# Sums of squares and output combinations by accumulating DMAs instead of VectorE additions

## The chip, the cores and the metric

The kernel runs on one core of one Trainium2 chip. The metric is the device time of one execution in microseconds (us); lower is better. A core has TensorE (PE, matmuls; its weight loads are listed as PEld), VectorE (DVE), ScalarE (ACT), GpSimd (POOL) and SyncE (SP), each with its own queue of instructions that it works off in order and with semaphores between them. Here SP issues all loads and stores; the DMA engines carry them out.

## The reference

Four batches of 6080 tokens with 256 channels go through an attention over channels and then through a two-layer network with squared ReLU:

```python
qn = q / (np.linalg.norm(q, axis=1, keepdims=True) + 1e-06)
kn = k / (np.linalg.norm(k, axis=1, keepdims=True) + 1e-06)
s = kn.transpose(0, 2, 1) @ qn / tau          # 256 x 256 per batch
a = np.exp(s - s.max(-1, keepdims=True))
a /= a.sum(-1, keepdims=True) + 1e-09
x = (v @ a).reshape(B * S, D)                 # (24320, 256)
h = np.maximum(x @ w_in, 0.0)                 # w_in: 256 x 2048
out = (h * h @ w_out).astype(np.float32)      # w_out: 2048 x 256
```

All of it is fp32. q, k and v are (4, 6080, 256).

## The kernel before

**Precision.** Every fp32 matrix is split into a high part and a low part (`_hi`, `_lo`), and a product is the sum of three: high by high, high by low, low by high. ScalarE makes the high part (a cast), VectorE the low part (the original minus the high part).

**Per batch: Gram matrix, softmax, folded weight.** `Gram` forms k^T q (tile `gram`) over chunks of tokens. A chunk is a tile `qk` of 128 partitions x (k or q) x 2 tokens x 256 channels, 128 x 1024 fp32 or 512 KB; with 6080 tokens there are 25 chunks: 0 to 22 are full, 23 has one token per partition, 24 has 64 partitions. The norms need the sums of squares of q and k over tokens. `squares` (ScalarE) squares a chunk, for later batches in place in its qk tile; `add_squares` adds the squares to the tile `acc`, chunk after chunk. `softmax_and_W` then adds acc's two halves (VectorE), sums them over the partitions by small matmuls (`ps_n`), forms the softmax, and multiplies it into w_in, which gives the folded weight `w_hi`, `w_lo` of the batch.

Batch 0 does this at the start (`start_first`). The first `HEAD = 6` chunks of batch 1 are loaded early and summed by `head_squares`. The rest of batch 1, and batches 2 and 3, run as the generator `attention(b)`, one piece of which is called per step of the main loop, beside the output blocks of the batch before. Per chunk it splits the qk tile into `qk_hi` and `qk_lo`, then calls `squares`, `add_squares` and, in the same piece, the load of the chunk after next (`g.load(c + QK_BUFS)`, `QK_BUFS = 2`): there are two qk buffers, so that load has to wait until the squares in the old chunk have been added. That is line 325 (k) and 326 (q) of the profile, on SP.

**Output blocks.** A batch's tokens are cut into 12 blocks, ten of 512 and two of 480. For a block there are 16 products with the folded weight (`first_product`: six matmuls into `ps_h`, then ScalarE's ReLU into `x`), two to a pair. `squares_and_sums` squares a pair (ScalarE), forms sums of quarters (VectorE) and splits them into `g_hi`, `g_lo`. Two pairs later `second_product` multiplies by w_out into `ps_o`. All blocks but the first two do it with seven products of half-size blocks instead of eight (`seven_products`), at the price of sums before and behind. The very last block does so for five of its eight pairs only (`SWITCH = 5`) and closes with plain products (`final_products`).

After a block's last pair, ScalarE copies the seven sums from `ps_o` into the tile `o` (128 x 7 x 256, one buffer, tag `o_sb`) in two copies, three slots and then four. `combine(b, n)` then turns the seven into the four quarters of the output, in five VectorE additions over three visits, and SP stores the quarters to `out_T` (line 841). The visits come from the list `late_work`, which the main loop looks at once per pair, before that step's `second_product`. For the last block the result stays in `o` for `final_products`.

**Order.** The main loop writes out by hand, step by step, what PE, VectorE, ScalarE and GpSimd get, and each keeps that order (`InProgramOrder`; so all their instructions have line 27). Semaphores and the order of SP's DMAs come from the framework: an instruction waits for whatever it reads or overwrites. GpSimd has nothing to do after setting up constants.

Of the kernel before, what the change touches and what calls it, by code (L numbers as in the profile page):

```python
# [14 lines left out]
ALU = mybir.AluOpType  # L15
# [15 lines left out]
def kernel(  # L31
# [21 lines left out]
    nc = tc.nc  # L53
    tensor, vector, scalar, pool_engine = (
        InProgramOrder(tc, e) for e in (nc.tensor, nc.vector, nc.scalar, nc.gpsimd)
    )
    P = 128
    B, N, C = q.shape
# [238 lines left out]
    HEAD = 6  # L297
# [3 lines left out]
    class Gram:  # L301
# [58 lines left out]
        def add_squares(self, c):  # L360
            p, jn, _ = self.q[c]
            if c in self.sq:
                a = self.acc[:p, :, :jn, :]
                vector.tensor_add(a, a, self.sq.pop(c)[:p, :, :jn, :])

    grams = {}

# [418 lines left out]
    def seven_products(b, n, r, part):  # L786
# [26 lines left out]
        if last:  # L813

            if part == 0:
                O[b, n] = pool.tile([P, 7, half], F32, tag="o_sb", name=f"o{b}_{n}", bufs=1)
            o, first = O[b, n], 1 - part
            scalar.copy(o[:, 3 * part : 3 * part + 4 - first, :], O.pop((b, n, part))[:, first:4, :half])
            if part:
                late_work.append(combine(b, n))  # L820

    def combine(b, n):

        t0, tn = blocks[n]
        half = tn // 2
        o = O.pop((b, n))
        both = lambda i: o[:, i : i + 1, :].broadcast_to([P, 2, half])
        vector.tensor_add(o[:, 1:4:2, :], o[:, 1:4:2, :], both(0))
        yield
        vector.tensor_add(o[:, 5, :], o[:, 5, :], o[:, 3, :])  # L830
        vector.tensor_add(o[:, 0, :], o[:, 5, :], o[:, 4, :])
        yield
        vector.tensor_add(o[:, 4, :], o[:, 4, :], o[:, 3, :])
        vector.tensor_add(o[:, 2:7:4, :], o[:, 2:7:4, :], o[:, 4:6, :])
        if (b, n) == order[-1]:
            final["sums"] = o
            return
        at = b * N + t0
        out = outT[:, at : at + tn].rearrange("(m p) t -> p m t", p=P)
        for m, k, slot in ((0, 0, 2), (0, 1, 1), (1, 0, 0), (1, 1, 6)):  # L840
            nc.sync.dma_start(out[:, m, k * half : (k + 1) * half], o[:, slot, :])
        yield

    late_work = []

    final = {}
# [68 lines left out]
    order = [(b, n) for b in range(B) for n in range(NB)]  # L915
# [20 lines left out]
    at = 0  # L936
# [13 lines left out]
    def then_sums():  # L950
        while grams[1].raws if B > 1 else False:
            yield
        yield from sums_of_w_out()

    sums = then_sums()
# [8 lines left out]
    for i in range(len(steps) + 2 * LAG):  # L964
        part = now["part"] = i % 2
        if i < len(steps):
            b, n, f = steps[i]
            at = b * NB + n
# [74 lines left out]
```

## Time and profile before

| | |
|---|---|
| timed runs | 2213.72 and 2215.77 us, median 2214.74 |
| span of the profiled execution, first to last instruction | 2211.6 us |
| PE busy | 2203.1 us |
| DVE busy | 1818.0 us |
| ACT busy | 1859.1 us |
| POOL busy | 0.7 us |
| DMA, mean | 67 GB/s |
| granted TensorE clock | 1.000 |

The page gives the profiled execution by its span; what lies around it, some 2 to 4 us by the timed runs, is not in the records. Busy time counts an engine's instructions but not the issuing of DMAs and the waiting for semaphores. A row of a group has line, engine, operation, tile written and tiles read, shapes, count, and then busy time, mean ns of one and the idle time in front of them. A row of a timeline has start, duration (both us), engine and operation. A row of DMAs has the size of one and the median time from its issue to its landing. A row of waits has who waited for whom, the total in us, how often, and the longest.

### The profile page before, as it was taken

What the parts mean: (1) busy time and instruction counts of PE and PEld (TensorE: products, weight loads), DVE (VectorE), ACT (ScalarE), POOL (GpSimd) and SP (SyncE); (2) the same over time, 40 slices, a digit from 0 to 9 for tenths busy, and PEclk for the clock granted to TensorE, in tenths of its full rate; (3) what the DMA queues carried; (4) which work ended last, traced back from release to release, by engine and by line L of the source; (5) the groups of instructions that cost most, each with busy time, mean ns of one, the idle gap of its engine ahead of it and who ended that gap; (6) DMA issues with size and microseconds to landing.
All of it is one profiled execution on the core that took longest, in us unless ns stands there. A gap on an engine that the chain in (4) does not pass through costs nothing.

```text
span 2211.6 us, 34981 instructions
## 1 busy us (share of the span) xinstructions
PE 2203.1 (100%) x13903; PEld 1985.0 (90%) x13903; DVE 1818.0 (82%) x2614; ACT 1859.1 (84%) x2347; POOL 0.7 (0%) x6
## 2 busy tenths in 40 slices
PE   9999999999999999999999999999999999999999
PEld 8789999988999999998999999999899988888898
DVE  6878888889888888878888888887888877787776
ACT  5788888888888888888878888888888888888887
POOL 0000000000000000000000000000000000000000
PEclk9999999999999999999999999999999999999999
DMA  9521122023421122210122122111103010010000
GB/s 342 179 77 39 61 77 65 27 76 109 157 86 58 60 62 71 63 60 21 36 95 86 60 66 76 58 53 60 33 24 115 22 36 20 22 37 20 20 28 19
DMA packets 82261, 148.03 MB, mean 67 GB/s; under 512 B 8368, under 2 KB 35760, under 8 KB 82096
## 3 DMA queue, kind: packets, MB, share of 16 engines
q1 hardware_dynamic: 82096, 145.79, 19.9%
q8 instruction: 109, 1.79, 0.3%
q14 instruction: 56, 0.46, 0.1%
HBM read 112.46 MB, written 33.29 MB: 66 GB/s over the span
## 4 chain that ended last, share of the span: by engine, by line
PE 92%; DVE 3%; DMA 2%; ACT 2%; issue 0%; SPq 0%; DVEq 0%; ACTq 0%
PE ps_h L27 46%; PE ps_o L27 41%; PE gram L27 4%; PE ps_w L27 2%; DMA qk<-in_k 1%; DVE g_lo L27 1%; DVE x L27 1%; ACT x L27 1%; DMA qk<-in_q 0%; DMA qk_heads<-in_q 0%; ACT g_hi L27 0%; DVE o L27 0%; DMA w_raw<-in_w_in 0%; DVE dec_m L27 0%; DMA wi_lo<-wi_kept 0%
## 5 line engine op out<-in xcount | busy, mean ns | idle before, releaser
L27 DVE TENSOR_TENSOR g_lo<-x,g_hi 128x768 fp32r<-128x768 f32 (+2 forms) x749 | 808.2, 1079 | 71.7 <-ACT g_hi L27 71.1
L27 DVE TENSOR_TENSOR x<-x 128x512 f32<-128x512 f32 (+1 forms) x1095 | 558.2, 510 | 244.0 <-ACT x L27 218.3
L27 ACT CAST g_hi<-x 128x768 fp32r<-128x768 f32 (+2 forms) x749 | 702.1, 937 | 42.8 <-DVE x L27 30.0
L27 ACT ACTIVATE x<-ps_h 128x512 f32<-128x512 f32 (+1 forms) x768 | 456.0, 594 | 248.7 <-PE ps_h L27 228.0
L27 PE MATMUL ps_h<-v_hi,w_hi 128*128 128x512 f32 (+1 forms) x1536 | 478.6, 393 | 0.0
L27 PE MATMUL ps_h<-v_hi,w_lo 128*128 128x512 f32 (+1 forms) x1536 | 477.9, 392 | 0.0
L27 PE MATMUL ps_h<-v_lo,w_hi 128*128 128x512 f32 (+1 forms) x1536 | 474.9, 390 | 0.0
L27 ACT ACTIVATE x<-x 128x1024 f32<-128x1024 f32 (+1 forms) x384 | 404.5, 1053 | 11.9
L27 PE MATMUL ps_o<-g_lo,wS_hi 128*128 128x256 f32 (+1 forms) x1460 | 407.6, 279 | 1.2 <-DVE g_lo L27 1.1
L27 PE MATMUL ps_o<-g_hi,wS_hi 128*128 128x256 f32 (+1 forms) x1460 | 406.1, 278 | 0.8 <-ACT o L27 0.8
L27 PE MATMUL ps_o<-g_hi,wS_lo 128*128 128x256 f32 (+1 forms) x1460 | 406.6, 278 | 0.0
L27 PEld LDWEIGHTS ps_h<-v_lo,w_hi 128*128 128x128 f32 x1536 | 287.9, 187 | 64.9
L27 PEld LDWEIGHTS ps_h<-v_hi,w_lo 128*128 128x128 f32 x1536 | 288.5, 188 | 62.4 <-DVE w_lo L27 0.3
L27 PE MATMUL ps_o<-g_hi,wo_hi 128*128 128x256 f32 (+2 forms) x1159 | 325.2, 285 | 0.6 <-ACT g_hi L27 0.6
L27 PE MATMUL ps_o<-g_hi,wo_lo 128*128 128x256 f32 (+2 forms) x1159 | 325.1, 285 | 0.0
L27 PE MATMUL ps_o<-g_lo,wo_hi 128*128 128x256 f32 (+2 forms) x1159 | 324.8, 285 | 0.1
L27 PEld LDWEIGHTS ps_o<-g_lo,wS_hi 128*128 128x128 f32 x1460 | 274.8, 188 | 17.9 <-DVE g_lo L27 2.1
L27 PEld LDWEIGHTS ps_o<-g_hi,wS_hi 128*128 128x128 f32 x1460 | 274.1, 188 | 17.2 <-ACT o L27 1.6
L27 PEld LDWEIGHTS ps_o<-g_hi,wS_lo 128*128 128x128 f32 x1460 | 274.4, 188 | 0.0
L27 PEld LDWEIGHTS ps_h<-v_hi,w_hi 128*128 128x128 f32 x1536 | 237.4, 188 | 3.6
L27 PEld LDWEIGHTS ps_o<-g_hi,wo_hi 128*128 128x128 f32 x1159 | 218.3, 188 | 15.7 <-ACT g_hi L27 1.0
L27 PEld LDWEIGHTS ps_o<-g_lo,wo_hi 128*128 128x128 f32 x1159 | 217.7, 188 | 15.2 <-DVE g_lo L27 0.5
(120 smaller groups left out, 1776.1 us busy)
## 6 DMA issues: line engine op xcount, KB each, us to landing
qk<-in_k SPq DMA_DIRECT2D x87, 256.0 KB, 2.8
qk<-in_q SPq DMA_DIRECT2D x87, 256.0 KB, 3.0
v<-in_vT SPq DMA_DIRECT2D x40, 512.0 KB, 3.8
out_T<-o SPq DMA_DIRECT2D x152, 128.0 KB, 1.7
wiS<-wi_sums_kept SPq DMA_DIRECT2D x24, 512.0 KB, 5.7
wi_hi<-wi_kept SPq DMA_DIRECT2D x16, 512.0 KB, 4.5
wi_lo<-wi_kept SPq DMA_DIRECT2D x16, 512.0 KB, 3.8
w_raw<-in_w_in SPq DMA_DIRECT2D x4, 1024.0 KB, 6.4
```

Of the source, the lines that this page charges most:

```text
L27: return lambda *args, **kwargs: self.tc.keep_in_program_order(issue(*args, **kwargs))
```

## The change

In batches after the first, `add_squares` for chunks from `HEAD` on no longer adds on VectorE: GpSimd issues a DMA from the squares (in the qk tile) to `acc` that adds to its destination. The first six chunks of every batch, and all of batch 0, stay on VectorE.

`combine` does the same for all blocks but the last: five accumulating DMAs within the tile `o`, issued by GpSimd over four visits, and the four stores in a fifth. The sums are arranged a little differently, so one output quarter ends in slot 5 instead of slot 0. The last block keeps the VectorE additions.

```diff
@@ add_squares @@
             if c in self.sq:
                 a = self.acc[:p, :, :jn, :]
-                vector.tensor_add(a, a, self.sq.pop(c)[:p, :, :jn, :])
+                if self.b == 0 or c < HEAD:
+                    vector.tensor_add(a, a, self.sq.pop(c)[:p, :, :jn, :])
+                else:
+                    pool_engine.dma_start(a, self.sq.pop(c)[:p, :, :jn, :], accum_op=ALU.add)
@@ combine @@
         both = lambda i: o[:, i : i + 1, :].broadcast_to([P, 2, half])
+        if (b, n) != order[-1]:
+            add = lambda at, what: pool_engine.dma_start(at, what, accum_op=ALU.add)
+            add(o[:, 1:4:2, :], both(0))
+            yield
+            add(o[:, 4, :], o[:, 3, :])
+            yield
+            add(o[:, 3, :], o[:, 5, :])
+            yield
+            add(o[:, 2:6:3, :], both(4))
+            add(o[:, 6, :], o[:, 3, :])
+            yield
+            at = b * N + t0
+            out = outT[:, at : at + tn].rearrange("(m p) t -> p m t", p=P)
+            for m, k, slot in ((0, 0, 2), (0, 1, 1), (1, 0, 5), (1, 1, 6)):
+                nc.sync.dma_start(out[:, m, k * half : (k + 1) * half], o[:, slot, :])
+            return
         vector.tensor_add(o[:, 1:4:2, :], o[:, 1:4:2, :], both(0))
         yield
         vector.tensor_add(o[:, 5, :], o[:, 5, :], o[:, 3, :])
...
         vector.tensor_add(o[:, 2:7:4, :], o[:, 2:7:4, :], o[:, 4:6, :])
-        if (b, n) == order[-1]:
-            final["sums"] = o
-            return
-        at = b * N + t0
-        out = outT[:, at : at + tn].rearrange("(m p) t -> p m t", p=P)
-        for m, k, slot in ((0, 0, 2), (0, 1, 1), (1, 0, 0), (1, 1, 6)):
-            nc.sync.dma_start(out[:, m, k * half : (k + 1) * half], o[:, slot, :])
-        yield
+        final["sums"] = o
```

## The prediction

> **What bounds the kernel now.** I read the page's busy line first, then the table of stretches, then what TensorE (PE) waited for.
>
> ```profile
> span 2211.6 us, 34981 instructions
> PE 2203.1 (100%) x13903; PEld 1985.0 (90%) x13903; DVE 1818.0 (82%) x2614; ACT 1859.1 (84%) x2347; POOL 0.7 (0%) x6
> ```
>
> PE is busy for all but 8.5 us of the span. VectorE (DVE), the engine that the change relieves, idles 18% of it, and GpSimd (POOL), which gets the new work, has six instructions in all. A busy PE could still be a slow one, so the next view is by stretch; its columns are the stretch, its length, the busy time of PE, PEld, DVE, ACT and POOL, the granted clock, the DMA share and GB/s.
>
> ```profile
> core 0: us, PE busy (x) PEld busy (x) DVE busy (x) ACT busy (x) POOL busy (x), PEclk, DMA share, GB/s
> 0.00:80.00 80.00, 77.25 (x344) 64.03 (x345) 60.05 (x78) 49.88 (x59) 0.70 (x6) 1.00 0.85 300
> ...
> 440.00:540.00 100.00, 98.06 (x618) 87.28 (x617) 88.92 (x153) 82.95 (x112) 0.00 (x0) 1.00 0.23 80
> ...
> 620.00:968.00 348.00, 348.00 (x2268) 316.13 (x2267) 296.08 (x402) 305.18 (x379) 0.00 (x0) 1.00 0.20 62
> ...
> 2170.00:2212.00 42.00, 37.75 (x231) 34.02 (x229) 24.39 (x38) 27.65 (x36) 0.00 (x0) 0.98 0.07 25
> ```
>
> Three stretches have PE idle: the start, 2.75 us (DMA share 0.85, and nothing of the change is there yet); 440 to 540, 1.94 us; and the end, 4.25 us, nearly all of it after the last matmul. In 620 to 968, a whole Gram stage with its squares, PE never stops, at clock 1.00. So VectorE can give back at most the middle one. What PE waited for after 80 us says the same:
>
> ```profile
> PE ps_o L27 <- DVE g_lo L27: 1.1, 2, 0.6
> PE ps_o L27 <- ACT o L27: 0.8, 2, 0.5
> ```
>
> Two waits on VectorE's low parts, two on ScalarE's copy of the output sums: 1.9 us together. This is the whole ceiling of a gain.
>
> **What goes from VectorE.**
>
> ```profile
> L27 DVE TENSOR_TENSOR acc<-acc,qk 128x1024 f32<-128x1024 f32 x63 | 76.9, 1221 | 12.2 <-ACT qk L27 12.2
> L27 DVE TENSOR_TENSOR o<-o 128x512 f32<-128x512 f32 x76 | 52.3, 688 | 1.3
> L27 DVE TENSOR_TENSOR o<-o 128x256 f32<-128x256 f32 x114 | 47.9, 420 | 1.3
> L27 DVE TENSOR_TENSOR o<-o 128x480 f32<-128x480 f32 x16 | 10.5, 655 | 0.3
> L27 DVE TENSOR_TENSOR o<-o 128x240 f32<-128x240 f32 x24 | 9.7, 403 | 0.3
> ```
>
> Of the 63 full chunk adds, chunks 6 to 22 of batches 1, 2 and 3 go: 17 x 3 = 51, by 1.221 us that is 62.3 us; the short chunks 23 and 24 of each batch go too, six adds of some 0.68 us, 4 us. Of the combinations, 46 blocks use seven products and only the last keeps its adds: all 76 and 114, 14 of 16 and 21 of 24, so 52.3 + 47.9 + 9.2 + 8.5 = 118 us. Together 184 us of 1818, which leaves VectorE at 1634 us, 74%. None of it is on the path outside 440 to 540, where the change removes about two blocks' adds (2 x 2.6 us). I credit half of the 1.94 us: **-1 us**.
>
> **What comes to POOL and the DMA engines.** 57 accumulations of squares and 45 x 5 of outputs, 282 DMAs. The trace has not one DMA issued by POOL and not one that accumulates, so their durations are bounded from SP's rows (size, us to landing):
>
> ```profile
> qk<-in_k SPq DMA_DIRECT2D x87, 256.0 KB, 2.8
> v<-in_vT SPq DMA_DIRECT2D x40, 512.0 KB, 3.8
> out_T<-o SPq DMA_DIRECT2D x152, 128.0 KB, 1.7
> w_raw<-in_w_out SPq DMA_DIRECT2D x4, 1024.0 KB, 5.4
> wi_sums_kept<-wiS_made SPq DMA_DIRECT2D x8, 512.0 KB, 2.6
> DMA to landing us min/median/max: 2.1/3.0/8.3
> ```
>
> (The last row is that of the qk tiles.) An accumulation reads source and destination, so I take the row with twice its bytes. A chunk of squares is 128 x 1024 fp32, 512 KB: between the 2.6 us of a plain store and the longest landing, 8.3 us; taken, as the 1 MB row, 5.4 us. A 256 KB step of the combination: 1.7 to 8.3, taken 3.8; a 128 KB step: 1.7 to 8.3, taken 2.8. The Trainium skill ("DMA: Bandwidth & Descriptors", Anatomy of one DMA, SWDGE path) fits a POOL-issued copy by 2.0 us plus bytes over 436 KB per us, which gives 3.2 us for 512 KB as an estimate; no run here shows one, and by it every cover below is wider still.
>
> *Squares.* What did take 1.22 us on VectorE now stands before a load, because the chunk after next lands in the buffer that the accumulation reads (two qk buffers). One of the closest places, ScalarE, VectorE and SP in turn:
>
> ```profile
> 676.02 1.05 ACT L27 CAST qk_hi<-qk 128x1024 fp32r<-128x1024 f32 x1
> 681.81 1.06 ACT L27 ACTIVATE qk<-qk 128x1024 f32<-128x1024 f32 x1
> 683.78 1.22 DVE L27 TENSOR_TENSOR acc<-acc,qk 128x1024 f32<-128x1024 f32 x1
> 685.02 0.34 SPq L325 DMA_DIRECT2D qk<-in_k  x1
> 685.41 0.42 SPq L326 DMA_DIRECT2D qk<-in_q  x1
> ...
> 699.87 1.04 ACT L27 CAST qk_hi<-qk 128x1024 fp32r<-128x1024 f32 x1
> ```
>
> The square ends at 682.87, the split of the chunk that this load brings starts at 699.87: 17.0 us. Two issues (0.8) and the landing (3.0) take 3.8, so 13.2 us are left for the accumulation; it needs 5.4, and if POOL stands first behind one combination step (3.8), 9.2. Cost nothing; without that cover each us would be ScalarE's, which is in order and has the next ReLU behind the split. Even 8.3 + 3.8 = 12.1 fits. SP waits longer at this load than before; behind it stand v loads and output stores, which have no deadline within a block (43 us by the copies below).
>
> *The new wait on VectorE.* At a batch's end the last, short accumulation (64 partitions) is followed by VectorE's sum of acc's halves, and behind that in its queue stand the low parts for PE.
>
> ```profile
> 430.85 0.62 ACT L27 ACTIVATE qk<-qk 64x512 f32<-64x512 f32 x1
> 438.04 0.68 DVE L27 TENSOR_TENSOR acc<-acc 128x512 f32<-128x512 f32 x1
> 440.36 0.28 PE L27 MATMUL ps_n<-ones,acc 128*128 128x1 f32 x2
> ```
>
> From the square's end, 431.47, to 438.04 are 6.6 us, for 128 KB (2.8). Cost nothing; at the upper end, 8.3, VectorE is held 1.7 us and the matmul at 440.36 starts nearly on time, three times in the run.
>
> *Combination.* Five VectorE adds over three visits become add 1, add 2, add 3, then adds 4 and 5 side by side, each waiting for the landing of the one before: 3.8 + 2.8 + 2.8 + 3.8 = 13.2 us, plus 0.3 for the fifth issue. The stores come one visit later in the program. Nobody waits for them but the next copy into the single o buffer, a block later; only in front of the last block, which closes its seven products after five of eight pairs, is that short:
>
> ```profile
> 668.51 1.01 ACT L27 COPY o<-ps_o 128x1024 f32<-128x1024 f32 x1
> 712.72 0.81 ACT L27 COPY o<-ps_o 128x768 f32<-128x768 f32 x1
> ...
> 2173.52 0.96 ACT L27 COPY o<-ps_o 128x960 f32<-128x960 f32 x1
> ...
> 2194.99 0.77 ACT L27 COPY o<-ps_o 128x720 f32<-128x720 f32 x1
> ```
>
> In the first pair 43.2 us lie between the copies; in the second, 2174.48 to 2194.99, 20.5 us: three stores' issues (0.34 each, as the loads') and a landing (1.7) leave 17.8, against 13.5. Cost nothing. Issuing costs POOL alone, whose six instructions all lie in the first stretch.
>
> **Sum.** -1 us on the span: 2210.6. The profiled span lies 3.1 us under the median of the timed runs, 2214.74 (2213.72 and 2215.77), so the median becomes 2213.7.
>
> **Rivals.**
>
> *A, accumulations slow enough to starve the splits (slower).* Place: the split of the chunk after next. It decides from 13.2 us on, 2.4 times what I take. For it: no row shows an accumulating DMA, nor how fast POOL hands one out. Against: the longest landing is 8.3 us. Price: in the quoted place two chunks take 23.85 us (676.02 to 699.87), but 25 chunks in the 348 us of that stage take 13.9 each, 27.8 for two, so the cover is 4 us longer on average and I take half the chunks to be as close as the quoted one. At 16 us the loss is 2.8 us x 51 x 1/2 = 71 us: 2285. Chance 0.12.
>
> *B, POOL and VectorE hold each other up.* VectorE's rows above all have two SBUF inputs. If such an instruction and POOL's preparing of a DMA exclude each other, each of 282 DMAs costs VectorE up to one long instruction, 1.22 us: 344 us for the 184 it lost, net +160, so 1978 of 2212, 89%. That is the share it had in 440 to 540 (88.92), where PE lost 1.94 us in 100. Over the 2000 us after 170 that makes 39 us at most, half of it as the value: +20, 2234. For it: the sharing can't be seen in a trace whose POOL works in the first stretch alone. Chance 0.10. The Trainium skill speaks on both sides: "SBUF — State Buffer", Who interferes with whom, says that a two-input VectorE instruction contends only with GpSimd instructions that read SBUF, and infers that preparing descriptors needs the write side; "GPSIMD Engine Reference", Key points, names two SBUF inputs as contention without that exception. No run here shows which.
>
> *C, the tail.* If a step takes 6 us, the chain before the last block takes 24 and the copy at 2194.99 waits 24 + 2.7 - 20.5 = 6.2 us with the last output matmuls behind it; with the credit, 2220. It decides from 4.4 us a step. Chance 0.14.
>
> *D, the change relieves something the trace hides.* Only if PE ran below its rate for VectorE's sake; the 348 us without a gap speak against it. That the adds would stay on VectorE I don't expect, and it would read as the time before. Chance of a gain above the ceiling 0.02.
>
> **Numbers.** The forecast has the remaining 0.62, at 2209 (the ceiling of the gain, the runs' own 1 us, some room) to 2218. Two per cent, about what a measurement of this kernel can tell from no change, is 44 us: slower begins at 2259. Only A (0.12) and B's upper tail (0.02) reach that: slower 0.14. Faster by 2% would need 23 times the ceiling: 0.01. The rest, 0.85, is within 2%. The range takes in the forecast, C and B up to its value: 2209 to 2236.
>
> **What would show it.** Right: DVE near 1634 us with PE still near 2203; the load at L325 waiting for a DMA into acc, landing under 13 us after the square; no ScalarE idle in front of qk_hi; the copy into o at the end not waiting for a store. For A: ScalarE's qk_hi idle on a qk load, and the span growing in Gram stages only. For B: VectorE's mean rows longer or its idle put down to POOL. For C: idle before the copy into o in the last 20 us alone. I am wrong in the core if PE shows idle in 620 to 968 without any of these, or if the span falls by more than 2 us.

## The result, and the profile after

The changed kernel takes 2233.66 us (two runs, 2232.69 and 2234.64) against 2214.74 us before: ratio 1.0088, 95% interval [1.0059, 1.0117]. It is 19 us slower, within the 2% that count as no change here, but not the 1 us faster of the forecast. The profiled execution has a span of 2230.9 us, 19.3 more than before, at a mean granted clock of 0.995. One execution of one kernel of the experiments (the eleventh blocks alone, 3762.76 us at a mean granted clock of 0.637) is in a slow state and is left out of that kernel's figures.

The head of the page after:

```profile
span 2230.9 us, 35335 instructions
...
PE 2208.5 (99%) x13903; PEld 1991.2 (89%) x13903; DVE 1666.6 (75%) x2332; ACT 1858.7 (83%) x2347; POOL 281.3 (13%) x288
```

VectorE is relieved by 151 us, and yet PE is slower: 5.4 us more busy, and idle for 22.4 us (2230.9 − 2208.5) where it was 8.5. The 13.9 us of idle time and the 5.4 us of busy time are the 19.3 us. The stretches after, in the columns of the table shown of before:

```profile
440.00:540.00 100.00, 100.00 (x640) 90.53 (x639) 88.00 (x150) 87.23 (x117) 12.16 (x12) 1.00 0.39 106
575.00:592.00 17.00, 14.53 (x98) 13.18 (x96) 13.48 (x22) 12.94 (x19) 3.90 (x4) 1.00 0.54 113
592.00:599.00 7.00, 4.67 (x22) 4.71 (x23) 2.11 (x6) 1.27 (x2) 0.00 (x0) 0.51 0.74 294
...
620.00:968.00 348.00, 348.00 (x2269) 316.10 (x2268) 261.20 (x347) 304.53 (x379) 52.71 (x55) 1.00 0.48 109
```

From 440 to 540 PE no longer stops (before: 98.06). The Gram stage from 620 to 968 is as full as it was, with the new DMAs in it. Of these stretches only 575 to 599 shows a loss: PE idles, and then runs at a granted clock of 0.51. Before, PE was busy there throughout, at 1.00:

```profile
592.00:599.00 7.00, 7.00 (x50) 6.56 (x49) 6.72 (x13) 5.03 (x7) 0.00 (x0) 1.00 0.35 110
```

What PE waited for after 80 us, longest first (the list before began with the waits for g_lo and o, which are gone):

```profile
PE ps_w L27 <- DMA wi_hi<-wi_kept: 15.4, 3, 5.7
```

Three waits, 15.4 us. `ps_w` is where the next batch's folded weight is formed. For that, w_in in high and low parts lies in HBM (`wi_kept`) and comes back piece by piece into `wi_hi` and `wi_lo`; SP issues each piece at line 235, once the piece before it has been read out of its buffer. This goes on during the eleventh block of batches 0, 1 and 2. SP's queue there, and the matmul that waits, after:

```profile
576.92 11.86 SPq L845 DMA_DIRECT2D out_T<-o  x4
588.84 0.44 SPq L235 DMA_DIRECT2D wi_lo<-wi_kept  x1
589.38 0.39 SPq L235 DMA_DIRECT2D wi_hi<-wi_kept  x1
...
594.33 0.55 PE L27 MATMUL ps_w<-wi_hi,eT_hi 128*128 128x256 f32 x1 [4.80 <-DMA wi_hi<-wi_kept]
```

and before:

```profile
582.32 0.32 SPq L235 DMA_DIRECT2D wi_lo<-wi_kept  x1
582.69 0.42 SPq L235 DMA_DIRECT2D wi_hi<-wi_kept  x1
583.22 0.84 SPq L291 DMA_DIRECT2D wiS<-wi_sums_kept  x2
584.15 6.08 SPq L841 DMA_DIRECT2D out_T<-o  x2
...
592.51 0.28 PE L27 MATMUL ps_w<-wi_hi,eT_hi 128*128 128x256 f32 x1
```

Before, the reload stands ahead of the stores in SP's queue; after, behind all four of them. In the program the stores have moved the other way: `combine` issues them on its fifth visit instead of its third, two visits later (the prediction says one). So the framework's order of SP's DMAs isn't the program's. One of the stores goes at 576.92; the other three wait for the chain of accumulations in `o`, which GpSimd issues:

```profile
573.14 1.20 POOL L27 DMA_DIRECT2D o<-o  x1 [24.47 <-ACT o L27]
577.15 0.91 POOL L27 DMA_DIRECT2D o<-o  x1 [2.81 <-DMA o<-o]
580.80 0.86 POOL L27 DMA_DIRECT2D o<-o  x1 [2.74 <-DMA o<-o]
583.65 2.13 POOL L27 DMA_DIRECT2D o<-o  x2 [1.99 <-DMA o<-o]
```

The last two land at about 587.5, the stores are out at 588.78, the reload starts at 588.84 and its second half at 589.38 lands 4.8 us later. Its buffer had been read by 579.3, so it started 9 to 10 us late, of which 4.8 show as PE's idle time. The same stands at 1147.47 (5.67 us) and 1699.79 (4.90 us). And the loss goes on after the wait:

```profile
592.03:598.85 6.82, 4.53 (x21) 4.56 (x22) 1.95 (x5) 1.27 (x2) 0.00 (x0) 0.50 0.75 299
598.86:605.68 6.82, 6.82 (x48) 6.40 (x47) 4.40 (x7) 3.95 (x5) 0.00 (x0) 1.00 0.15 40
```

For 6.83 us, from late in the wait until 4.3 to 5.0 us behind it, the granted clock is 0.50, at each of the three places. That is where PE's additional busy time lies.

### The profile page after: what moved, and what is told of

It is laid out like the page before. It is cut to its first block, busy times and chain, and to the rows that moved or that the text cites. A ratio compares the mean times of both kernels' runs of the same rounds, so it can differ in the third digit from the quotient of the medians.

```text
span 2230.9 us, 35335 instructions
## 1 busy us (share of the span) xinstructions
PE 2208.5 (99%) x13903; PEld 1991.2 (89%) x13903; DVE 1666.6 (75%) x2332; ACT 1858.7 (83%) x2347; POOL 281.3 (13%) x288
## 4 chain that ended last, share of the span: by engine, by line
PE 95%; DMA 3%; DVE 1%; ACT 1%; SPq 0%; issue 0%; DVEq 0%; ACTq 0%
PE ps_h L27 47%; PE ps_o L27 42%; PE gram L27 4%; PE ps_w L27 2%; DMA qk<-in_k 1%; DMA wi_hi<-wi_kept 1%; DMA o<-o 1%; DMA qk<-in_q 0%; DMA qk_heads<-in_q 0%; ACT x L27 0%; DMA w_raw<-in_w_in 0%; DVE dec_m L27 0%; DVE g_lo L27 0%; PE ps_n L27 0%; ACT sq L27 0%
## 5 line engine op out<-in xcount | busy, mean ns | idle before, releaser
L27 POOL DMA_DIRECT2D o<-o x225 | 239.7, 1177 | 1300.9 <-ACT o L27 950.0
```

Source lines behind the costliest of these rows:

```text
L27: return lambda *args, **kwargs: self.tc.keep_in_program_order(issue(*args, **kwargs))
```

## The experiments

The theory: the loss comes from the combination alone, in three blocks of 45, through the order of SP's queue and not through GpSimd, the DMA engines or VectorE; without it the change would gain some 3 us, where PE waited for g_lo and o. The rivals: the squares (the forecast's A), GpSimd and VectorE holding each other up (B), the DMA traffic as such. Each ratio is against executions of the kernel before that were taken with that experiment; their medians are 2213.27 to 2213.50 us.

**1. The two halves apart.** The squares by DMA with the old `combine`; and the new `combine` with the squares on VectorE:

```diff
-                if self.b == 0 or c < HEAD:
+                if True:
                     vector.tensor_add(a, a, self.sq.pop(c)[:p, :, :jn, :])
```

Expected of the squares alone:

> Theory (the loss is three stalls of TensorE in the fold of the next batch's weight, where the reload of w_in's second group stands behind output stores that wait for the combination's DMAs in SP's queue): the accumulations of squares have no part in it, all output adds are back on VectorE, so no idle in front of ps_w and a time within 3 us of before (ratio 0.999 to 1.001). Rival (the added DMA traffic as such slows loads and with them TensorE): the 57 accumulations of squares are 27 of the 69 MB that were added, so about 0.4 of the 19 us stay, +7 us (ratio 1.003).

Expected of the combination alone:

> The other half alone: squares back on VectorE, output combination by DMAs. Theory: all of the loss, +18 to +22 us (ratio 1.008 to 1.010), with three idle times of 4 to 6 us in front of ps_w. Rival (traffic as such): 0.6 of it, +12 us (ratio 1.005).

Measured: the squares alone 2214.09 us, ratio 1.0003 [0.9994, 1.0012]; the combination alone 2233.16, ratio 1.0089 [1.0075, 1.0103]. The squares cost nothing and bring nothing. The stretch 440 to 540 with the squares alone, and PE's longest wait with the combination alone:

```profile
440.00:540.00 100.00, 98.02 (x621) 87.34 (x620) 88.91 (x153) 82.96 (x112) 0.00 (x0) 1.00 0.22 79
```

```profile
PE ps_w L27 <- DMA wi_hi<-wi_kept: 17.1, 3, 5.9
```

**2. The eleventh blocks taken out, or alone.** In the first kernel the change stays whole, but the eleventh block of each batch is combined on VectorE. In the second, the kernel before, only the eleventh blocks of batches 0 to 2 are combined by DMAs, 15 DMAs in all:

```diff
-        if (b, n) != order[-1]:
+        if (b, n) != order[-1] and n != NB - 2:
...
```

```diff
+        if n == NB - 2 and b < B - 1:
+            add = lambda at, what: pool_engine.dma_start(at, what, accum_op=ALU.add)
...
```

Expected of the change without the eleventh blocks:

> The change as a whole, except that the combination of the eleventh block of each batch (three of them beside a fold) stays on VectorE: 42 of 45 combinations and all squares go by DMA. Theory: the three stalls are gone and the clock stays at 1.0 throughout; what is left is the gain in 440 to 540 us, so 0 to -3 us against before (ratio 0.9985 to 1.0005). Rival (traffic as such): 42 of 45 of the output accumulations and all squares remain, so +18 us (ratio 1.008).

Expected of the eleventh blocks alone:

> The kernel before, and only the combination of the eleventh block of batches 0 to 2 by DMAs: 15 of the 282. SP's order here again has the four stores in front of the reload. Theory: the whole loss from these 15, three idle times of about 5 us plus the half clock behind each (some 2.3 us), and none of the gain in 440 to 540, so +20 to +23 us (ratio 1.009 to 1.0105), more than the change itself. Rival (traffic as such): 15 of 282 DMAs, +1 us (ratio 1.0005).

Measured: without them 2209.97 us, ratio 0.9986 [0.9977, 0.9995], and no wait of ps_w; alone 2237.32, 2239.51 and 2241.76, ratio 1.0118 [1.0101, 1.0134]. So 41 of the 45 combinations do no harm (the eleventh block of the last batch, beside which nothing is folded, is left out too), and the three do all of it. They lose 26 us alone, more than the 20 to 23 expected: the waits are longer (17.6 us against 15.4), and PE's busy time grows by 8.1 us (2203.1 to 2211.2), 2.7 at each place. Why both are larger here stays open. With the three alone the old waits are still there:

```profile
PE ps_w L27 <- DMA wi_hi<-wi_kept: 17.6, 3, 6.1
PE ps_o L27 <- DVE g_lo L27: 1.2, 3, 0.6
...
PE ps_o L27 <- ACT o L27: 0.8, 2, 0.5
```

By traffic as such these fifteen DMAs should have cost 1 us, and GpSimd issues only 15 here instead of 282; what is left is the place where they stand.

**3. SP's queue alone.** Two ways to let the reload pass, with the accumulations kept. First, the change with nothing altered but the engine that issues the four stores:

```diff
-                nc.sync.dma_start(out[:, m, k * half : (k + 1) * half], o[:, slot, :])
+                pool_engine.dma_start(out[:, m, k * half : (k + 1) * half], o[:, slot, :])
```

> Every accumulating DMA of the change stays, only the four stores behind each combination are issued by GpSimd instead of SP. Theory (the harm is the place in SP's queue): the reload no longer has a waiting store in front of it, it goes out within 3 us of the matmuls that release its buffer, no idle in front of ps_w, 0 to -3 us against before (ratio 0.9985 to 1.0005). Rivals (traffic, or the accumulations disturbing VectorE): nothing of theirs is changed, +19 us (ratio 1.009).

Second, the first of the five additions back on VectorE in the eleventh blocks, after which the reload stands ahead of the stores in SP's queue:

```diff
-            add(o[:, 1:4:2, :], both(0))
+            if n == NB - 2:
+                vector.tensor_add(o[:, 1:4:2, :], o[:, 1:4:2, :], both(0))
+            else:
+                add(o[:, 1:4:2, :], both(0))
```

> The change, but in the eleventh block of each batch the first of the five adds is made by VectorE; the other four stay DMAs, and the stores stay on SP. With this the reload stands in front of the four stores in SP's queue, as before the change. Theory (the order in the queue): no idle in front of ps_w, 0 to -4 us (ratio 0.998 to 1.000), although the chain of DMAs beside the fold is still three landings long. Rival (the length of the chain, whatever the order): one of four steps less, some 4 us less delay of about 6.5, so idle of 1 to 2 us three times with or without a drop of the clock: +1 to +9 us.

Measured: stores by GpSimd 2210.09 us, ratio 0.9985 [0.9976, 0.9994]; first addition by VectorE 2210.72, ratio 0.9988 [0.9978, 0.9997]. Both lose the wait. The reload and the matmul with the stores by GpSimd:

```profile
578.91 0.32 SPq L235 DMA_DIRECT2D wi_lo<-wi_kept  x1
579.32 0.38 SPq L235 DMA_DIRECT2D wi_hi<-wi_kept  x1
...
589.10 0.28 PE L27 MATMUL ps_w<-wi_hi,eT_hi 128*128 128x256 f32 x1
```

and with the first addition on VectorE, where SP waits as long as ever for its stores, but with the reload already out:

```profile
579.34 0.32 SPq L235 DMA_DIRECT2D wi_lo<-wi_kept  x1
579.75 0.38 SPq L235 DMA_DIRECT2D wi_hi<-wi_kept  x1
580.23 0.84 SPq L291 DMA_DIRECT2D wiS<-wi_sums_kept  x2
581.17 15.42 SPq L848 DMA_DIRECT2D out_T<-o  x4
```

The first keeps all five accumulations. The second keeps four of five and the stores on SP, which are out only by 596.59, later than in the changed kernel (588.78); the reload is ahead of them, and PE does not wait. So neither the accumulations nor the length of their chain costs the time, but the reload's place in SP's queue. Against the change itself, GpSimd's stores take away 15.4 us of waits and 6.4 us of PE's busy time (2208.5 to 2202.1); by that the half clock costs some 2.1 us each time. Why the framework puts the stores first in the changed kernel stays open.

**4. Where the gain comes from.** The kernel before with the eighth and ninth block of batch 0 combined by DMAs; and the combination by DMAs in all blocks, stores by GpSimd, with the squares on VectorE:

```diff
+        if (b, n) in ((0, 7), (0, 8)):
+            add = lambda at, what: pool_engine.dma_start(at, what, accum_op=ALU.add)
...
```

Expected of the two blocks:

> The kernel before, with the output sums combined by accumulating DMAs in two blocks only, the eighth and ninth of the first batch; no fold of a next batch's weights stands in either, and the squares stay on VectorE. If the kernel after earns its gain where TensorE waited for VectorE and ScalarE between 440 and 540 us (1.1 and 0.8 us of waits, 98.06 of 100 us busy there), the two blocks that stand in that stretch earn it all: about 2210 to 2212 us, ratio 0.9985 to 0.9995, TensorE busy for 100 of the 100 us and neither wait left. If the gain is spread over the whole of the span, two blocks of 64 earn nothing that can be measured: 2214, ratio 1.000.

Expected without the squares:

> The combination by accumulating DMAs with the four output stores issued by GpSimd, and the squares of q and k on VectorE as in the kernel before. If the squares by DMA add nothing to the gain, this stands where the changed kernel with GpSimd's stores stood (ratio 0.9985): 2210 to 2211 us, ratio 0.998 to 0.999, no wait of ps_w for wi_hi. If VectorE needs both reliefs for the gain, it is back at 2213 to 2215, ratio 1.000, with TensorE's waits for g_lo and o between 440 and 540 us.

Measured: two blocks 2210.36 us, ratio 0.9986 [0.9977, 0.9995]; all blocks without the squares 2210.21, ratio 0.9985 [0.9976, 0.9994]. Two blocks earn all that 45 earn (the 64 in the expectation is a slip). With the two blocks alone:

```profile
440.00:540.00 100.00, 100.00 (x640) 90.55 (x639) 88.00 (x149) 87.20 (x117) 10.31 (x10) 1.00 0.37 103
```

The 100 us hold 22 matmuls more than before (640 against 618). At 100/640 = 0.156 us each that is some 3.4 us (roughly: with the squares alone, and the same waits, the stretch shows 621). The spans differ by 2.7 (2211.6 and 2208.9), the medians by 3.1.

**5. How much slower an accumulation of squares may be.** The squares alone by DMA, each full chunk added twice, and four times (the diff, against the squares alone by DMA, shows four). The norms, and with them the outputs, are then others than the reference's.

```diff
-                    pool_engine.dma_start(a, self.sq.pop(c)[:p, :, :jn, :], accum_op=ALU.add)
+                    sq = self.sq.pop(c)[:p, :, :jn, :]
+                    for _ in range(4 if jn == J else 1):
+                        pool_engine.dma_start(a, sq, accum_op=ALU.add)
```

Expected of twice:

> Squares by DMA alone (output adds on VectorE), and each full chunk is added to acc twice, one DMA waiting for the landing of the other, so the norms of batches 1 to 3 are not the reference's. This doubles the time between the square and the load: 2 x 4.7 = 9.4 us, against the 13.2 us of cover in the prediction. Expected if that cover is right: no change (ratio 0.999 to 1.001). If the real cover is half of it: splits late by 2 to 3 us in half of 51 chunks, +60 us.

Expected of four times:

> The same with four additions of each full chunk, again with other norms than the reference's: 4 x 4.7 = 18.8 us, 5.6 over the cover of 13.2. By the price of rival A in the prediction (half of 51 chunks late by the excess) +143 us, ratio 1.065, with ScalarE idle in front of qk_hi on the load. If SP's queue and the slack behind hide more than the prediction allowed: under +40 us.

Measured: twice 2213.84 us, ratio 1.0002 [0.9992, 1.0012]; four times 2618.58, ratio 1.183 [1.1806, 1.1854]. With two, ScalarE waits for a load before one of the 51 splits only, for 0.5 us. With four:

```profile
POOL acc L27 <- DMA acc<-qk: 905.9, 200, 6.5
...
ACT qk_hi L27 <- DMA qk<-in_q: 431.0, 51, 13.5
```

GpSimd waits 4.5 us for an addition to land (905.9/200) before it issues the next, which takes it 0.86; a step in the chain is 5.4 us, four are 21.6. But a chunk comes every 13.9 us (25 in the 348 us of a stage, as the prediction counts). So the additions of one chunk aren't done when those of the next are due: 200 of the 210 wait for the landing of the one before, most first additions of a chunk among them. The square that ends at 1004.41 gets its first addition at 1019.17, behind the four of the chunk before:

```profile
1003.36 1.05 ACT L27 ACTIVATE qk<-qk 128x1024 f32<-128x1024 f32 x1
1019.17 0.86 POOL L27 DMA_DIRECT2D acc<-qk  x1 [4.22 <-DMA acc<-qk]
```

The chain sets the pace: (21.6 − 13.9) × 51 = 393 us, near the 405 measured. The 143 expected took the four additions as a delay of each chunk by itself, against a cover of 13.2 us, and half of the chunks as late; ScalarE waited before all 51, 8.45 us on average (431.0/51), and the clock fell as well (0.84 in 1000 to 1080). That 21.6 − 8.45 = 13.1 is so near to the cover of 13.2 is luck and doesn't confirm it, since the 8.45 come from the pace.

## Why the prediction was wrong, point by point

**The bound.** Right as far as it went: outside the start, 440 to 540 and the end, PE had nothing to gain. That the relief helps there and nowhere else is shown by the two blocks. The ceiling was 1.9 us, read from idle time alone; the two blocks gave 2.7 us by the spans and 3.1 by the medians. The four matmuls right behind the waits took 0.38 to 0.39 us, where their groups have a mean of 0.28, so some 0.4 us of the loss lay inside PE's busy time, and the idle time was no ceiling. Where the rest comes from stays open. That "the span falls by more than 2 us", named as a sign of being wrong in the core, did happen once the queue was mended.

**What goes from VectorE.** 184 us forecast, 151 us measured. The instructions went as counted, but durations overlap: the trace of before has an `o` addition of 0.69 us at 690.02 and the next instruction at 690.63. So the durations of a group add up to more than the busy time that goes with it (33 us over 282 instructions is 0.12 us each; 0.08 at this place). Nothing hung on it.

**Durations of accumulations.** DMA rows after:

```profile
acc<-qk POOLq DMA_DIRECT2D x51, 512.0 KB, 4.6
...
o<-o POOLq DMA_DIRECT2D x76, 256.0 KB, 3.8
out_T<-o SPq DMA_DIRECT2D x152, 128.0 KB, 1.8
o<-o POOLq DMA_DIRECT2D x114, 128.0 KB, 4.0
```

Taken were 5.4, 3.8 and 2.8: the first and second good, the third low, though with the squares on VectorE the 128 KB steps have medians of 2.8 and 2.9. The chain takes 14.3 us at the place above (573.14 to about 587.5) and 13.6 at a quicker one (1180.95 to 1194.59); the forecast's 13.5 was good.

**Squares.** Right: the load of the chunk after next is issued 5.7 us after the square's end (885.96 to 891.64 at one chunk), for a cover of 13.2. The additions made twice bear the cover out: at one chunk they hold the load until 11.3 us after the square (870.57 to 881.84), with 17.0 us to the split as in the forecast's place, and ScalarE's splits waited 0.5 us for loads in the whole run. Rival A did not come. Its price leaves out that the accumulations of successive chunks go one behind another: past the chunks' pace of 13.9 us each further us is lost at every chunk. The new wait at a batch's end is hidden as forecast: from the square's end to VectorE's sum of the halves are still 6.6 us (978.71 to 985.29).

**Rival B** did not come: VectorE's rows have not grown, and PE lost nothing in 620 to 968. The forecast's 2234 for it is near the measured 2233.66, and the range took that time in, by luck: the mechanism is another.

```profile
L27 DVE TENSOR_TENSOR g_lo<-x,g_hi 128x1024 fp32r<-128x1024 f32 x320 | 391.4, 1223 | 115.9 <-ACT g_hi L27 115.3
```

(1220 ns before.) The Trainium skill ("SBUF — State Buffer", Who interferes with whom), by which a two-input VectorE instruction contends only with GpSimd instructions that read SBUF, and which infers that preparing descriptors needs the write side, agrees with this row.

**Rival C** did not come: the chain in front of the last block starts at 2193.98, its stores are out by 2209.2, and the copy into `o` stands at 2214.20 with no wait in front.

```profile
2193.98 1.20 POOL L27 DMA_DIRECT2D o<-o  x1 [26.60 <-ACT o L27]
```

```profile
2214.20 0.77 ACT L27 COPY o<-ps_o 128x720 f32<-128x720 f32 x1
```

**The step that failed** is the sentence on what stands in SP's queue: "behind it stand v loads and output stores, which have no deadline within a block", and its twin on the stores, "Nobody waits for them but the next copy into the single o buffer". With these the forecast put SP's waits at no cost. The first leaves the reloads of w_in out of the queue. The second is true of the stores' data. But the stores also hold SP's queue while they wait, and behind them, in three blocks, stands the reload of w_in with a deadline of some 10 us (from 579.3, when its buffer had been read, to 589.53, when PE needs it). What the runs showed in place of "no cost" are PE's three waits of 15.4 us in all and the half clock behind them, 6.4 us. The forecast asked who waits for the stores' result, and not who stands behind the stores. Waiting at the stores is not new, and no view of totals would have told:

```profile
SPq L845 <- DMA o<-o: 1043.5, 98, 32.2
```

and before:

```profile
SPq L841 <- DVE o L27: 1059.3, 124, 30.2
```

SP waited for about as long before. What is new is that at three places of 45 a reload that PE needs soon stands behind that wait. SP's timeline of before shows line 235 beside the stores there, so something with a deadline shares the queue. That the order would turn could not be read from it, but a price could: a chain of 13.5 us in front of a reload that had 5 us of slack before (issued at 582.69, landed in the 4.7 us that this one took at 587.4, used at 592.51). Three times some 13.5 − 5 = 8.5 us, less what the chain has already done when the reload is due, would have been a rival of up to 25 us.

## What to carry to other kernels

When work moves from an engine to a chain of DMAs, look not only at what waits for the chain's end, but also at what is queued behind that waiter: list, at each place, the loads that share the in-order queue with it, each with its deadline. Issue stores that wait for such a chain from another queue than loads with a deadline; here that alone turned +19 us into −3 (by GpSimd, with nothing else changed). And before relieving an engine everywhere, find the stretch where its lateness shows: two blocks of 45 earned all of the gain.

## What the runs showed of the hardware

**A wait of 5 us costs more than itself.** PE's three waits of 4.80, 5.67 and 4.90 us were each followed by a granted clock of 0.50, for 6.83 us every time, beginning 2.5 to 3.2 us into the wait (592.03 against 589.53 at the first). Against the kernel with the stores from GpSimd that adds some 2.1 us to each; of the two kernels with the squares on VectorE, stores from SP (PE busy 2206.7 us) and from GpSimd (2201.3), it is 1.8. That is about a third of the wait. The Trainium skill ("TensorE: Matmul & The Clock Gate", Part 1: The HAM clock gate) has half rate after at least one idle window of about 3.4 us, and windows that run freely. The 6.83 us are two such windows, and the three drops begin 552.96 us apart (592.03, 1144.99, 1697.95), 162 times 3.413 us, which agrees. But only 2.5 to 3.2 us of each wait lie in front of the drop, so a window of 3.4 us that ends there held 0.2 to 0.9 us of matmuls and was not idle throughout.

**The time of an accumulating DMA grows little with its size here.** In the changed kernel 128 KB took 4.0 us to land, 256 KB 3.8 and 512 KB 4.6 (medians). With the squares on VectorE the 128 KB steps took 2.8 to 2.9 us; those of 256 KB stayed at 3.8. GpSimd is busy while it issues one, 1.18 us for a step in `o` and 0.89 us for the squares on average (239.7 us in 225, 50.8 us in 57). A store of 128 KB takes 3.3 us to land when GpSimd issues it (four in a row) and 1.8 when SP does.
